# Two evictions per expert block: each half of layer 2 read out behind its own 24 matmuls

## Chip, cores and metric

The kernel runs on one core of one Trainium2 chip. The metric is device time in microseconds (us) of one execution; several executions are timed and their median counts. One further execution was recorded by the hardware profiler, and all rows below are of that one.

## What is computed

The input x is 8 batches of 2496 rows of 256 numbers. A two-dimensional Fourier transform is taken per batch and its real part kept, which gives 19968 rows (tokens). Each token goes to one of 8 experts, the one with the largest logit, and is written back at its own place:

```python
X = np.fft.fft(np.fft.fft(x, axis=1), axis=2).real
logits = X @ w_gate + modality_bias[modality_id]
e_idx = argmax(logits)                    # one expert per token
gate_w = softmax(logits)[e_idx]
out[mask] = gate_w[mask] * (relu(X[mask] @ w1[e]) @ w2[e])   # w1 256 x 1024, w2 1024 x 256
```

## The kernel before, in words

Two kinds of work share the engines. The **stream** makes the transform of one batch after the other (`fold`, `stage1`, `stage23`), computes the logits, gives each token a place in the list of its expert (`route`) and scatters the token rows to DRAM (`scatter`, line 726, an indirect DMA issued by GpSimd). The **expert blocks** (`block`, lines 1068 to 1153) take 256 rows (or, at the very end, 128 rows) of one expert from DRAM and run both layers on them. The first blocks run while the stream still makes later batches; later only blocks are left: first those of 256 rows, then those of 128.

A block of 256 rows does the following.

- **Loads**, issued by the sync engine: the expert's weights `w1` and `w2` (lines 1097, 1098, three slots each), the rows transposed as `xT` (line 1100, three buffers), and each row's place in the output and gate as `ig` (line 1103, four buffers).
- **Layer 1** (lines 1110 to 1127): four groups of 24 matmuls at 128 columns or, with 256 rows, of 12 matmuls at 256 columns; 48 matmuls in all. The three products of high and low fp16 parts are added up in a PSUM tile `psm` (three buffers). ScalarE writes the high part of the relu to `H` (line 1124), VectorE the low part (line 1125). `H` has two buffers.
- **Layer 2** (lines 1130 to 1140): for each half `tg` of 128 rows 24 matmuls at 256 columns into `po[:, tg, :]`. Both halves stand in one PSUM tile `pso` of 2 x 256 fp32 per partition, and the pool has one buffer for it (line 259).
- **Gates' product** `gs` (line 1144): one small VectorE instruction, held behind the block's own last relu instruction (`low`) by `issue_after`.
- **Eviction and scatter** (lines 1145 to 1152): for each half ScalarE reads `po[:, tg, :]`, multiplies by the gate and writes `ob` (four buffers), and GpSimd issues the indirect DMA that scatters `ob` to the output.

`block` is a generator. `blocks` and `spec_blocks` run the first part (loads, layer 1) of block b+1 ahead of the second part (layer 2, evictions) of block b, so the program's text has the order: layer 1 of b+1, layer 2 of b, layer 1 of b+2, layer 2 of b+1. `self.ob` is the last eviction issued in the text; the relu instructions of the next layer 1 in the text come behind it on ScalarE (lines 1122 to 1124).

The text's order is not the order on the engines. The kernel is built with

```python
    with tile.TileContext(nc, schedule_with_timeline_sim=True) as tc:
```

(line 1333): at build time a scheduler puts each engine's instructions in an order, by their place in the text and by estimated times at which their operands and buffers come free, and adds the semaphore waits that the accesses to each tile need. On the chip each engine then works through its fixed order. `issue_after` and `high_priority` are the kernel's means to bend that order.

Of the kernel before, what the change touches and what calls it, by code (L numbers as in the profile page):

```python
# [13 lines left out]
F32 = mybir.dt.float32  # L14
# [4 lines left out]
ALU = mybir.AluOpType  # L19
# [3 lines left out]
P = 128  # L23
B, N, D = 8, 2496, 256
TOK = B * N
E, F = 8, 1024
# [222 lines left out]
class Kernel:  # L249
# [818 lines left out]
    def block(self, S, ti, i, o=0, n=0, ex=None, slot=0, load=False):  # L1068

        keep = self.hold  # L1070
        self.hold = ()
        nc, t, p, tc = self.nc, self.t, self.mo, self.tc
        V = nc.vector
        NT = S // P
        ns = self.nslot
        sl = (self.off + i) % ns if ex is None else slot
        first = i < ns
        if ex is None:
            w = i % ns
            i = o + sum((n - j + ns - 1) // ns for j in range(w)) + i // ns  # L1080
        self.nblk += 1
        w1, w2 = self.w1[sl], self.w2[sl]
        kw = {}
        with ExitStack() as st:
            for x in keep + tuple(self.loads[-2:-1]):
                st.enter_context(tc.issue_after(x))
            ro = nc.sync.value_load(ti[0:1, 0, i:i + 1], min_val=0, max_val=DUMP)
            if ex is None:
                ee = nc.sync.value_load(ti[0:1, 1, i:i + 1], min_val=0, max_val=E - 1)
                if not first:  # L1090
                    kw = dict(cond=nc.sync.value_load(ti[0:1, 2, i:i + 1], min_val=0, max_val=1), cond_hint=False)
        if load:
            nc.sync.dma_start(w1, t["w16"][ex, :, 0:4 * F])
            nc.sync.dma_start(w2, t["w16"][ex, :, 4 * F:WROW])
        if ex is None:
            wsrc = t["w16"][ds(ee, 1)].rearrange("a p f -> (a p) f")
            nc.sync.dma_start(w1, wsrc[:, 0:4 * F], **kw)
            nc.sync.dma_start(w2, wsrc[:, 4 * F:WROW], **kw)
        xT = p.tile([P, 4, S], I16, name=f"xT{S}", tag="xT", bufs=3)
        r1 = nc.sync.dma_start_transpose(xT, t["xd"][ds(ro, S), 0:512])  # L1100
        xT = xT.bitcast(F16)
        ig = p.tile([P, NT, 2], F32, name=f"ig{S}", bufs=4)
        r2 = nc.sync.dma_start(ig.bitcast(I16), t["xd"][ds(ro, S), 512:516].rearrange("(t p) c -> p t c", p=P))
        self.loads.append(r2.ins)
        self.gather_dep(r1.ins)
        self.gather_dep(r2.ins)
        H = p.tile([P, 2, 8, S], F16, name=f"H{S}", tag="H", bufs=2)
        w1v = w1.rearrange("p (h k f) -> p h k f", h=2, k=2)
        NF = 512 // S
        for f0 in range(0, 8, NF):  # L1110
            ps = self.psm.tile([P, NF, S], F32, name="psm")
            for q in range(NF):
                ft = slice((f0 + q) * P, (f0 + q + 1) * P)
                k = 0
                for h, kt, xs in ((0, 0, 0), (0, 0, 2), (1, 0, 0), (0, 1, 1), (0, 1, 3), (1, 1, 1)):
                    with ExitStack() as st:
                        for x in keep:
                            st.enter_context(tc.issue_after(x))
                        l1 = nc.tensor.matmul(ps[:, q, :], w1v[:, h, kt, ft], xT[:, xs, :], start=k == 0, stop=k == 5).ins  # L1119
                    k += 1  # L1120
            with ExitStack() as st:
                if self.ob is not None:
                    st.enter_context(tc.issue_after(self.ob))
                nc.scalar.activation(H[:, 0, f0:f0 + NF, :], ps, AF.Relu)  # L1124
            self.mark = V.scalar_tensor_tensor(H[:, 1, f0:f0 + NF, :], ps, 0.0, H[:, 0, f0:f0 + NF, :], ALU.max, ALU.subtract).ins  # L1125
            if S == 256 and f0 % 4 == 0:
                self.tick(self.mark)
        self.l1, low = l1, self.mark
        yield
        w2v = w2[:, 0:4 * F].rearrange("p (h f d) -> p h f d", h=2, d=D)  # L1130
        po = self.pso.tile([P, NT, D], F32, name="pso")
        for tg in range(NT):
            k = 0
            for ft in range(8):
                for hh, wh in ((0, 0), (0, 1), (1, 0)):
                    with ExitStack() as st:
                        if S == P and k == 0:
                            st.enter_context(tc.issue_after(self.l1))
                        nc.tensor.matmul(po[:, tg, :], H[:, hh, ft, tg * P:(tg + 1) * P], w2v[:, wh, ft, :], start=k == 0, stop=k == 23)  # L1139
                    k += 1  # L1140
        gs = p.tile([P, NT], F32, name=f"gs{S}", bufs=3)
        with ExitStack() as st:
            st.enter_context(tc.issue_after(low))
            V.tensor_scalar(gs, ig[:, :, 1], w2[:, 4 * F:4 * F + 2].bitcast(F32), None, ALU.mult)
        for tg in range(NT):
            ob = p.tile([P, D], F32, name="ob", bufs=4)
            self.ob = nc.scalar.activation(ob, po[:, tg, :], AF.Identity, scale=gs[:, tg:tg + 1]).ins  # L1147
            ins = nc.gpsimd.indirect_dma_start(  # L1148
                out=t["out"], out_offset=bass.IndirectOffsetOnAxis(ap=ig.bitcast(I32)[:, tg, 0:1], axis=0),
                in_=ob, in_offset=None, bounds_check=TOK - 1, oob_is_err=False).ins  # L1150
            tc.declare_no_dep(ins, group="out_w", reason="rows are disjoint")
            tc.add_to_no_dep_group("out_w", ins)
        yield
# [189 lines left out]
```

## Time and profile before

| what | value |
|---|---|
| median of 3 timed runs | 1066.68 us (1066.59 to 1068.08) |
| profiled execution, its own time | 1056.95 us |
| its span, first to last instruction | 1055.2 us |
| TensorE matmul (PE) busy | 1009.6 us, 96% of the span |
| VectorE (DVE), ScalarE (ACT), GpSimd (POOL) busy | 532.3, 468.1, 363.2 us |
| layer 2's matmuls (L1139) | 3864, 452.2 us busy |
| layer 1's matmuls (L1119) | 4368, 457.7 us busy |
| evictions (L1147) | 161, 68.7 us busy |
| output scatters (L1148) | 161, 160.5 us busy on POOL |

How to read it: an engine is busy while an instruction of its own executes; PE, DVE, ACT and POOL work side by side, and SP issues most DMAs. Matmuls are pipelined: the start-to-start distance of two in a row is less than the duration given for one, so the time of a run of matmuls is read from the start of its first to the start of what follows. In a row of the timeline the bracket gives how long the engine stood idle before, and which instruction of which engine released it; a row without a bracket followed the one before it without a pause worth a mention. "x36" means 36 instructions in a row.

### The profile page before, as it was taken

The numbers are of one execution on the slowest core, as the hardware profiler recorded it, in microseconds if no ns is written. First come the engines' busy times: TensorE is split into PE (matmuls) and PEld (weight loads), VectorE is DVE, ScalarE is ACT, GpSimd is POOL, SyncE is SP. The second block draws the span as 40 slices with busy tenths as digits, with TensorE's granted clock in tenths as the row PEclk, the third lists the DMA queues.
The fourth block names the chain that finished last, engine by engine and source line by source line (L and its number), as shares of the span: only waits on it lengthen the run. The fifth ranks groups of instructions, "written<-read, shape, count | busy, mean of one in ns | idle before, by whom it ended". The sixth has DMA issues, their size and how long they took to land.

```text
span 1055.2 us, 25891 instructions
## 1 busy us (share of the span) xinstructions
PE 1009.6 (96%) x9910; PEld 906.9 (86%) x9910; DVE 532.3 (50%) x1567; ACT 468.1 (44%) x910; POOL 363.2 (34%) x353
## 2 busy tenths in 40 slices
PE   6979999999999998999999999999999999999996
PEld 6858778898899887988998898888888888898896
DVE  2848857577785576667654346522222222222221
ACT  4765566465555456436443334242323232332232
POOL 0066831227414444443333333444443121221111
PEclk9999999999999999999999999999999999999999
DMA  9836948458448949679764883789678887495972
GB/s 325 321 122 199 381 121 293 102 168 294 154 108 278 294 162 301 200 253 303 230 197 142 234 226 97 203 229 291 186 224 232 250 258 203 135 289 133 252 199 38
DMA packets 149724, 227.64 MB, mean 216 GB/s; under 512 B 116309, under 2 KB 117375, under 8 KB 132695
## 3 DMA queue, kind: packets, MB, share of 16 engines
q1 hardware_dynamic: 133031, 183.75, 60.2%
q0 software_dynamic: 16560, 42.15, 11.0%
q8 instruction: 80, 1.31, 0.5%
q14 instruction: 53, 0.43, 0.1%
HBM read 191.77 MB, written 62.48 MB: 241 GB/s over the span
## 4 chain that ended last, share of the span: by engine, by line
PE 74%; issue 11%; DMA 6%; POOL 3%; ACT 2%; DVE 2%; another core or an unknown queue 1%; SPq 0%; POOLq 0%; ACTq 0%
PE pso L1139 32%; PE psm L1119 32%; DMA XM<-x 3%; POOL out L1148 2%; DMA wa<-w 2%; PE psf L591 2%; PE psf L547 2%; PE psf L578 2%; PE psf L573 2%; PE psf L544 1%; PE psf L593 1%; DMA pack<-c_pack 1%; POOL xd L726 0%; DVE XM L405 0%
## 5 line engine op out<-in xcount | busy, mean ns | idle before, releaser
L1119 PE MATMUL psm<-xT,w 128*128 128x256 f16 (+1 forms) x4368 | 457.7, 261 | 8.0 <-DVE H L1125 2.8
L1139 PE MATMUL pso<-w,H 128*128 128x256 f16 x3864 | 452.2, 273 | 4.6 <-issue 2.4
L1119 PEld LDWEIGHTS <-w 128*128 128x128 f16 x4368 | 384.7, 98 | 50.0 <-issue 7.7
L1139 PEld LDWEIGHTS <-H 128*128 128x128 f16 x3864 | 375.0, 98 | 52.0 <-issue 9.2
L1125 DVE SCALAR_TENSOR_TENSOR H<-psm,H 128x512 f16<-128x512 f32 x322 | 219.3, 688 | 358.0 <-ACT H L1124 289.4
L1148 POOL DMA_INDIRECT out<-ob,ig x161 | 160.5, 997 | 499.2 <-ACT ob L1147 470.3
L1124 ACT ACTIVATE H<-psm 128x512 f16<-128x512 f32 x322 | 189.6, 597 | 256.0 <-PE psm L1119 186.5
L1147 ACT ACTIVATE ob<-pso,gs 128x256 f32<-128x256 f32 x161 | 68.7, 470 | 189.9 <-PE pso L1139 165.0
L726 POOL DMA_INDIRECT xd<-rp,dsti x88 | 101.6, 1155 | 114.6 <-DVE rm L233 49.8
L726 POOL DMA_INDIRECT xd<-rm,dsti x88 | 92.3, 1048 | 61.4 <-issue 20.8
L525 DVE SCALAR_TENSOR_TENSOR T<-psf,T 120x280 f16<-120x280 f32 (+2 forms) x95 | 43.4, 464 | 36.0 <-ACT T L524 35.2
L897 DVE SCALAR_TENSOR_TENSOR w<-wa,wsc,w 128x512 f16<-128x512 f32 (+1 forms) x52 | 42.5, 867 | 9.8 <-ACT w L890 9.6
L524 ACT ACTIVATE T<-psf 120x280 f16<-120x280 f32 (+2 forms) x95 | 38.7, 423 | 13.6 <-PE psm L1119 5.3
L578 PE MATMUL psf<-m2u,T 128*120 128x280 f32 x132 | 38.4, 414 | 2.3 <-ACT T L520 0.9
L547 PE MATMUL psf<-c,XM 128*128 128x132 f32 x240 | 31.9, 295 | 7.3 <-DMA c<-c_c 7.0
L591 PE MATMUL psf<-T,pack 120*128 120x145 f16 x330 | 34.5, 224 | 4.0 <-ACT T L524 1.6
L547 PEld LDWEIGHTS psf<-c,XM 128*128 128x128 f32 x240 | 30.7, 206 | 7.6 <-DMA XM<-x 7.0
L890 ACT ACTIVATE w<-wa,wsc 128x1024 f16<-128x1024 f32 (+1 forms) x24 | 33.4, 1426 | 2.2 <-DVE wsc L413 1.0
L525 DVE SCALAR_TENSOR_TENSOR rp<-psf,rp 128x256 f16<-128x256 f32 x55 | 22.9, 417 | 19.5 <-ACT rp L524 12.3
L573 PE MATMUL psf<-pack,T 128*120 128x144 f16 x330 | 31.9, 229 | 0.7 <-issue 0.7
L520 ACT COPY T<-psf 120x280 f32<-120x280 f32 (+2 forms) x57 | 22.7, 409 | 20.5 <-PE psf L578 9.3
L593 PE MATMUL psf<-T,pack 120*128 120x145 f32 (+1 forms) x132 | 24.1, 306 | 6.3 <-ACT T L520 3.7
(189 smaller groups left out, 611.3 us busy)
## 6 DMA issues: line engine op xcount, KB each, us to landing
w<-w SPq DMA_DIRECT2D x80, 1028.0 KB
w<-w SPq DMA_DIRECT2D x80, 1024.0 KB
XM<-x SPq DMA_DIRECT2D x14, 1280.0 KB
wa<-w SPq DMA_DIRECT2D x16, 1024.0 KB
out<-ob,ig POOLq DMA_INDIRECT x161
XM<-x SPq DMA_DIRECT2D x2, 768.0 KB
xT<-xd SPq DMA_TRANSPOSE x91
xd<-rp,dsti POOLq DMA_INDIRECT x88
```

Source lines behind the costliest of these rows:

```text
L525: self.mark = self.nc.vector.scalar_tensor_tensor(dst[:, 1], ps, scale, dst[:, 0], ALU.mult, ALU.subtract).ins
L547: self.staged = nc.tensor.matmul(o, src[:, k, i0 + i, :], self.c1[:, i1 + i, :], start=k == 0, stop=k == 1).ins
L573: nc.tensor.matmul(oh, T1[h][:, a, g, :], self.m2h[h][:, w], start=h + k == 0, stop=h * k == 2, skip_group_check=True)
L578: nc.tensor.matmul(ps[0:120, 0:280], T1[h][:, g, :], self.m2u[h], start=h == 0, stop=h == 1)
L591: nc.tensor.matmul(ps3[0:P, cols], self.e3h[:, a, j, :], T2[:, w, cols], start=k == 0, stop=k == 2)
L726: i = self.nc.gpsimd.indirect_dma_start(out=self.t["xd"], out_offset=bass.IndirectOffsetOnAxis(ap=at, axis=0), in_=row, in_offset=None, bo ...
L1119: l1 = nc.tensor.matmul(ps[:, q, :], w1v[:, h, kt, ft], xT[:, xs, :], start=k == 0, stop=k == 5).ins
L1124: nc.scalar.activation(H[:, 0, f0:f0 + NF, :], ps, AF.Relu)
L1125: self.mark = V.scalar_tensor_tensor(H[:, 1, f0:f0 + NF, :], ps, 0.0, H[:, 0, f0:f0 + NF, :], ALU.max, ALU.subtract).ins
L1139: nc.tensor.matmul(po[:, tg, :], H[:, hh, ft, tg * P:(tg + 1) * P], w2v[:, wh, ft, :], start=k == 0, stop=k == 23)
L1147: self.ob = nc.scalar.activation(ob, po[:, tg, :], AF.Identity, scale=gs[:, tg:tg + 1]).ins
L1148: ins = nc.gpsimd.indirect_dma_start(out=t["out"], out_offset=bass.IndirectOffsetOnAxis(ap=ig.bitcast(I32)[:, tg, 0:1], axis=0), in_=ob, i ...
```

## The change

The gates' product is written ahead of layer 2, and the second loop over the halves is gone: eviction and scatter of a half stand in the loop that makes it, behind its own 24 matmuls and ahead of those of the other half. No instruction is added or taken away. In a block of 128 rows there is one half only, and nothing but the place of the gates' product changes.

```diff
         w2v = w2[:, 0:4 * F].rearrange("p (h f d) -> p h f d", h=2, d=D)
         po = self.pso.tile([P, NT, D], F32, name="pso")
+        gs = p.tile([P, NT], F32, name=f"gs{S}", bufs=3)
+        with ExitStack() as st:
+            st.enter_context(tc.issue_after(low))
+            V.tensor_scalar(gs, ig[:, :, 1], w2[:, 4 * F:4 * F + 2].bitcast(F32), None, ALU.mult)
         for tg in range(NT):
             k = 0
             for ft in range(8):
...
                         nc.tensor.matmul(po[:, tg, :], H[:, hh, ft, tg * P:(tg + 1) * P], w2v[:, wh, ft, :], start=k == 0, stop=k == 23)
                     k += 1
-        gs = p.tile([P, NT], F32, name=f"gs{S}", bufs=3)
-        with ExitStack() as st:
-            st.enter_context(tc.issue_after(low))
-            V.tensor_scalar(gs, ig[:, :, 1], w2[:, 4 * F:4 * F + 2].bitcast(F32), None, ALU.mult)
-        for tg in range(NT):
             ob = p.tile([P, D], F32, name="ob", bufs=4)
             self.ob = nc.scalar.activation(ob, po[:, tg, :], AF.Identity, scale=gs[:, tg:tg + 1]).ins
             ins = nc.gpsimd.indirect_dma_start(
```

## Rows read from the trace of the kernel before

**Rows 1.** The page's busy time: engine, us, share of the span, instructions.

```profile
PE 1009.6 (96%) x9910; PEld 906.9 (86%) x9910; DVE 532.3 (50%) x1567; ACT 468.1 (44%) x910; POOL 363.2 (34%) x353
```

**Rows 2.** Stages: length, busy PE, PEld, DVE, ACT, POOL; granted clock; DMA share, GB/s.

```profile
100.00:600.00 500.00, 482.24 (x4689) 430.46 (x4689) 330.58 (x982) 262.21 (x515) 200.98 (x191) 0.99 0.72 224
...
700.00:900.00 200.00, 200.00 (x1835) 179.26 (x1833) 56.31 (x98) 62.30 (x116) 67.12 (x69) 1.00 0.82 234
```

**Rows 3.** Timeline, one block's cycle: start, length, engine, line, operation, tiles, count, idle before.

```profile
801.63 4.09 PE L1119 MATMUL psm<-xT,w 128*128 128x256 f16 x36
...
803.83 0.69 DVE L1125 SCALAR_TENSOR_TENSOR H<-psm,H 128x512 f16<-128x512 f32 x1 [2.99 <-ACT H L1124]
...
805.57 1.15 PE L1139 MATMUL pso<-w,H 128*128 128x256 f16 x9
...
806.55 1.47 PE L1119 MATMUL psm<-xT,w 128*128 128x256 f16 x12
...
807.86 4.42 PE L1139 MATMUL pso<-w,H 128*128 128x256 f16 x39
...
809.30 0.22 DVE L1144 TENSOR_SCALAR gs<-ig,w 128x2 f32<-128x2 f32 x1
...
812.12 4.09 PE L1119 MATMUL psm<-xT,w 128*128 128x256 f16 x36
...
812.37 0.84 ACT L1147 ACTIVATE ob<-pso,gs 128x256 f32<-128x256 f32 x2 [3.71 <-PE pso L1139]
...
813.12 0.97 POOL L1148 DMA_INDIRECT out<-ob,ig  x1 [8.23 <-ACT ob L1147]
```

**Rows 4.** Lines 1144 and 1147: forms of the gates' product; what ended ScalarE's idle time.

```profile
L1144 DVE TENSOR_SCALAR gs<-ig,w x91: 204/220/378, 107.5 to 1042.9; 128x2 f32<-128x2 f32 x70, 128x1 f32<-128x1 f32 x21
...
  PE pso L1139: 165.0, 66
```

**Rows 5.** Timeline, the last two blocks of 128 rows.

```profile
1041.49 2.78 PE L1139 MATMUL pso<-w,H 128*128 128x256 f16 x24
...
1044.31 0.47 ACT L1147 ACTIVATE ob<-pso,gs 128x256 f32<-128x256 f32 x1 [2.02 <-PE pso L1139]
1044.84 2.78 PE L1139 MATMUL pso<-w,H 128*128 128x256 f16 x24 [0.56 <-ACT ob L1147]
```

**Rows 6.** Timeline, first block: PE, then ACT; last a window's row, columns as rows 2.

```profile
114.46 0.38 PE L1139 MATMUL pso<-w,H 128*128 128x256 f16 x2
...
118.86 2.12 PE L1139 MATMUL pso<-w,H 128*128 128x256 f16 x14 [1.44 <-ACT ob L1147]
120.78 2.75 PE L1119 MATMUL psm<-xT,w 128*128 128x256 f16 x12
...
117.99 0.82 ACT L1147 ACTIVATE ob<-pso,gs 128x256 f32<-128x256 f32 x2
...
120.80:123.30 2.50, 2.50 (x13) 1.74 (x12) 2.50 (x10) 2.12 (x4) 1.92 (x2) 0.50 1.04 337
```

**Rows 7.** Timeline, three late evictions: layer 2's last matmuls, then their eviction.

```profile
351.44 4.42 PE L1139 MATMUL pso<-w,H 128*128 128x256 f16 x39
...
358.78 0.82 ACT L1147 ACTIVATE ob<-pso,gs 128x256 f32<-128x256 f32 x2
...
411.00 1.80 PE L1139 MATMUL pso<-w,H 128*128 128x256 f16 x15
...
415.46 0.82 ACT L1147 ACTIVATE ob<-pso,gs 128x256 f32<-128x256 f32 x2
...
652.99 1.91 PE L1139 MATMUL pso<-w,H 128*128 128x256 f16 x16
...
657.98 0.82 ACT L1147 ACTIVATE ob<-pso,gs 128x256 f32<-128x256 f32 x2
```

**Rows 8.** PE's waits over the whole span: us in total, times, longest.

```profile
PE psm L1119 <- DVE H L1125: 2.8, 2, 2.5
```

## The prediction

> **What bounds the kernel now.** I read the page first: TensorE is busy for 1009.6 us of the 1055.2 us span, twice as long as any other engine [rows 1]. A share over the whole span hides stages, so next come the windows. From 700 to 900 us, where only blocks of 256 rows run, PE is busy 200.00 us of 200 [rows 2]: nothing that shortens ScalarE's or GpSimd's work can be felt there. From 100 to 600 us, with the stream beside the blocks, PE stands idle for 500 - 482.24 = 17.8 us [rows 2]; that is all there is to gain, apart from the start and the end, which the change doesn't touch.
>
> The timeline of one cycle [rows 3] gives the order on PE: 36 matmuls of layer 1, 9 of layer 2, 12 of layer 1, 39 of layer 2, and again from 812.12, so 812.12 - 801.63 = 10.49 us for 96 matmuls, 0.109 us each, with no gap. Two things are to be seen in it. The first half's 24 matmuls are the 9 and 15 of the 39; they end at about 807.86 + 15 x 0.109 = 809.5. Yet ScalarE, idle for 3.71 us, starts the first eviction only at 812.37, behind the 48th matmul, and then does both in 0.84 us. So the program's guards treat `pso` as one thing: a reader waits for every matmul written ahead of it, whichever half it makes.
>
> **The change, part by part.** Reckoned on the profiled execution's own 1056.95 us; the median of the timed runs, 1066.68, lies 9.73 above it, and I add that difference at the end. About 0.2% (2.1 us) is what a measurement here can tell from no change.
>
> *Gates' product moved ahead of layer 2.* In the cycle it runs at 809.30 for 0.22 us, 3 us ahead of the eviction at 812.37, on a VectorE that is busy 56.31 us of 200 [rows 2, 3]. In both texts it waits for the block's own last relu, not for layer 2: 0. Its reader comes up to 2.8 us earlier, at 809.6, and 809.52 is still in time; without that cover at most its 0.22 us would add to each first eviction, less than what covers the boundary (below).
>
> *Scatter moved.* The first half's indirect DMA can leave GpSimd some 2.6 us earlier; GpSimd stood idle 8.23 us before it [rows 3], and no PE time hangs on it. The token scatters on the same queue may change places with it; each takes as long as before. 0. SyncE issues nothing new; the slots of `w2`, `ig` and `H` come free when the second half ends, later by whatever is put between the halves, some 1.3 us. What waits for them is for later blocks, with two to four buffers and a cycle of 10.49 us each: 0; without that cover the 1.3 us would show per block.
>
> *The eviction moved between the halves: a new wait.* By the same guard the second half's first matmul, now written behind the first half's eviction, must wait for it, since both are on `pso`. The product has 70 forms of two columns and 21 of one [rows 4], so there are 70 such boundaries. Its price stands at the kernel's end, where the last two blocks have nothing between them: 24 matmuls, eviction at 1044.31 for 0.47 us, the next 24 at 1044.84, PE idle 0.56 us [rows 5]. The 24 behind it take 2.78 us, as those before: this gap doesn't lower the clock. Queued behind the waiting matmul is all of PE's work, so an uncovered boundary costs 0.56 us: from 0 to 70 x 0.56 = 39 us.
>
> What covers it is layer 1 of block b+2: in the cycle it starts at 812.12 without a wait, so its rows and weights are there, and I take it that they are 2.6 us sooner too; `psm` has three buffers. That the build-time order pulls later work into a wait it foresees is in the cycle: the 9 matmuls of layer 2 ahead of layer 1's last 12 stand where it expected `psm` to be full. It overestimates such chains: VectorE had freed that buffer at 803.83 + 0.69 = 804.52, over 1 us before the 36 were through [rows 3]. A chain of one eviction should get 0.56 / 0.109 = 6 matmuls at least, and rather one group of 12 (1.31 us). I take **0 for the pure block stage**, being nearest to that row.
>
> In the mixed stage ScalarE isn't always free. Of 91 blocks 66 found it idle and waiting for PE [rows 4]; in the others it came from other work. The four latest first evictions, counted from layer 2's last matmul: 114.84 to 117.99 (3.15) [rows 6], 355.86 to 358.78 (2.92), 412.80 to 415.46 (2.66), 654.90 to 657.98 (3.08) [rows 7]. Before, 48 matmuls of layer 2 and then 36 of layer 1 (3.9 us) ran without that eviction; only in the first did PE wait for it, 1.44 us, and the 12 matmuls after that pause took 2.75 us, against 1.47 for 12 in the cycle [rows 3, 6]: the granted clock was 0.50 there, 1.2 instead of 2.4 GHz. With the change an eviction that late stands between the halves. Beyond a cover of 1.31 the four cost 1.84 + 1.61 + 1.35 + 1.77 = 6.6 us, and if each also drops the clock, 4 x (2.75 - 1.47) = 5.1 more: bounds 0 and 11.7. A gain is not excluded (below). I take half of 6.6, 3.3 us, as an estimate: ScalarE's order is written anew with this eviction in it, and part of the work that held it will come behind.
>
> Sum: 0 + 0 + 0 (block stage) + 3.3 = +3.3, 1060.25 us for a profiled run, **1070.0 us** on the median's scale.
>
> **A rule weighed.** The trace shows an eviction of one half waiting for the matmuls of the other [rows 3]. The Trainium skill, "PSUM — Partial Sum Buffer", section "PSUM bank collisions raise a hardware error", says that TensorE and ScalarE may not be on one bank of the same partitions at once, disjoint columns included, and advises to read another bank while matmuls run. The trace agrees, as far as the 2.87 us from 809.5 to 812.37 tell. By the rule alone each boundary stops PE, the second rival's 39 us; by the cycle's row it is filled, 0.
>
> **The rivals.** *All covered, nothing measurable*, 1066.7: the mixed stage's evictions find other filler too, the stream's matmuls. For it: 66 of 91 on time. Against: the four late ones.
>
> *The boundary is not filled*: PE stops 0.56 us 70 times, 1066.7 + 39 = 1106. It decides if the order puts no layer-1 matmul between the halves. For it: the guard [rows 3, 5]. Against: the 9 matmuls pulled forward.
>
> *Faster*: ScalarE no longer does 0.84 us of evictions in a row; behind the second half 0.47 is left, so relu and `psm` come 0.37 us sooner. If that, and a first eviction at 110 us rather than 118, removes the waits on `psm` (2.8 us) [rows 8] and on `pso` with its slow matmuls (1.44 + 1.28) [rows 6], 5.5 us go: 1061.2. It decides where ScalarE reaches the first eviction before its long operations. Against: it needs ScalarE exactly where it was late.
>
> *It doesn't do what it says*: with other work ahead in ScalarE's order the first eviction still comes behind the whole of layer 2. Then nothing moves; counted in the first rival.
>
> **How the numbers follow.** Small loss 0.33, all covered 0.32, not filled 0.10, faster 0.25. Slower by over 0.2% is 0.33 + 0.10 = 0.43, within 0.2% 0.32, faster 0.25. The forecast is the small loss, 1070.0. Its own upper bound is 1066.7 + 11.7 = 1078.4, and the lesser late ones that I didn't sum lie beyond it, so I end the range at 1080; downward it reaches to the faster case, 1061.5. Left out are the unfilled boundaries (0.10) and gains beyond 5 us (under 0.10).
>
> **What would show it.** In the timeline of 700 to 900 us: 24 matmuls of layer 2, about 12 of layer 1, 24 of layer 2, each eviction alone, 0.47 us behind its half, PE still 200.00 busy, the cycle still 10.49. In PE's waits: `pso` on ScalarE's `ob`, a handful of times between 100 and 660 us, a few us in total; many short ones of 0.56 mean the second rival. A lower PE idle from 100 to 600 than 17.8 means the faster one. I am wrong at the root if the second half starts while its neighbour is being read, or if the cycle changes.

## The result and the profile after

The changed kernel takes 1082.94 us (median of four runs, 1079.64 to 1084.78) against 1067.38 for the kernel before (four runs on the same chip, 1066.59 to 1069.95): the ratio is 1.0141, 95% interval 1.0098 to 1.0183. The change costs 15.6 us where 3.3 was forecast, and the time lies above the range's upper end of 1080. Measured twice more, on two chips, the loss was 0.9% and 1.0% (below). The sign was right, the size not.

The page's busy time of the changed kernel, the answer to [rows 1]:

```profile
span 1081.2 us, 25863 instructions
...
PE 1012.3 (94%) x9910; PEld 906.4 (84%) x9910; DVE 526.1 (49%) x1567; ACT 460.8 (43%) x910; POOL 357.3 (33%) x353
```

The same instructions, and PE busy for only 2.7 us more: the loss is for the most part not work but PE standing still. The stages, with the columns of [rows 2]:

```profile
100.00:600.00 500.00, 462.82 (x4494) 410.68 (x4493) 320.58 (x969) 250.56 (x498) 187.51 (x182) 0.98 0.69 212
...
700.00:900.00 200.00, 199.05 (x1820) 177.59 (x1818) 56.66 (x108) 60.57 (x118) 69.03 (x71) 1.00 0.82 239
```

From 700 to 900 us PE is busy nearly as before (199.05 against 200.00, and 15 matmuls fewer, about 1.6 us at 0.109 each). From 100 to 600 us it is idle for 500 - 462.82 = 37.2 us, where it was 17.8 [rows 2]. So the pure block stage all but carried the change, and the stage in which stream and blocks share the engines did not.

A cycle of the pure block stage, PE and then ScalarE, to hold against [rows 3]:

```profile
761.35 2.78 PE L1143 MATMUL pso<-w,H 128*128 128x256 f16 x24
763.97 1.36 PE L1119 MATMUL psm<-xT,w 128*128 128x256 f16 x11
765.17 2.78 PE L1143 MATMUL pso<-w,H 128*128 128x256 f16 x24
767.79 2.89 PE L1119 MATMUL psm<-xT,w 128*128 128x256 f16 x25
770.52 1.25 PE L1143 MATMUL pso<-w,H 128*128 128x256 f16 x10
...
764.22 0.47 ACT L1146 ACTIVATE ob<-pso,gs 128x256 f32<-128x256 f32 x1 [4.20 <-issue]
...
769.30 0.47 ACT L1146 ACTIVATE ob<-pso,gs 128x256 f32<-128x256 f32 x1 [3.15 <-PE psm L1119]
```

Counted through the trace, 24 by 24, the run at 761.35 is the second half of one block and that at 765.17 the first half of the next; the eleven of layer 1 stand between two blocks. Between the halves of a block stand 25: from 767.79 until the second half's first matmul at 770.52. The first half is through at 767.95 (765.17 + 2.78), its eviction begins at 769.30 and is over at 769.77, 0.75 us before the second half starts. That is the forecast's picture with twice its fill; behind the forecast's 12 matmuls, 1.31 us, PE would have waited for an eviction that comes so late. From the 48th block on 21 of 23 boundaries between halves have 25 matmuls in them, the other two 31.

PE's waits over the whole span, in us, times and longest, first those of before that stand beside [rows 8], then after:

```profile
PE psm L1119 <- DMA w<-w: 2.4, 2, 1.3
PE pso L1139 <- issue: 2.4, 5, 1.1
...
PE pso L1139 <- ACT ob L1147: 2.0, 2, 1.4
PE psm L1119 <- issue: 1.7, 3, 0.8
```

```profile
PE pso L1143 <- issue: 13.3, 9, 10.3
PE psm L1119 <- issue: 8.0, 12, 1.1
PE psm L1119 <- DVE H L1125: 6.9, 6, 1.7
...
PE pso L1143 <- ACT ob L1146: 4.8, 7, 1.1
PE psm L1119 <- DMA w<-w: 4.2, 3, 1.7
```

Three waits that the profile can name grew: `pso` on the eviction from 2.0 to 4.8, `psm` on VectorE's relu from 2.8 [rows 8] to 6.9, `psm` on weights from 2.4 to 4.2, together 8.7 us. "Issue", time for which the profile shows no releaser, grew from 11.1 to 27.0 over all lines. The largest piece of it is one stop, on PE, ScalarE and VectorE at once, in the timeline of 113 to 132 us (behind it a window's row, columns as [rows 2]):

```profile
130.42 0.97 POOL L726 DMA_INDIRECT xd<-rm,dsti  x1 [0.30 <-issue]
130.69 0.47 ACT L1146 ACTIVATE ob<-pso,gs 128x256 f32<-128x256 f32 x1 [15.05 <-remote]
...
131.22 1.65 PE L1143 MATMUL pso<-w,H 128*128 128x256 f16 x7 [10.28 <-issue]
...
131.69 0.69 DVE L1125 SCALAR_TENSOR_TENSOR H<-psm,H 128x512 f16<-128x512 f32 x1 [11.43 <-issue]
```

```profile
131.22:135.22 4.00, 4.00 (x21) 2.84 (x20) 1.38 (x5) 1.47 (x3) 2.12 (x3) 0.55 0.30 111
```

The 24 matmuls that this eviction reads were over by 116.9, and it comes 13.8 us later, while GpSimd goes on issuing token scatters. PE goes on just behind it, and its seven matmuls then take 1.65 us; seven take 0.92 in a row further below (at 479.88). The last row is the window of PE's first 4 us after the stop: the granted clock is 0.55, near the lower of its two levels (1.2 of 2.4 GHz), after 10 us in which PE stood still.

One caution on the scale. The profiled execution of before, 1056.95 us, lies 10.4 below its runs' median, that of after, 1082.95, on its own. Their difference of 26 us overstates the 15.6 of the medians, so a second pair of profiles is compared below. It is from two chips, on which the kernel before ran alike (medians 1044.16 and 1043.44).

### The profile page after: what moved, and what is told of

The parts are those of the page before. It is cut to its first block, busy times and chain, and to the rows that moved or that the text cites. A ratio compares the mean times of both kernels' runs of the same rounds, so it can differ in the third digit from the quotient of the medians.

```text
span 1081.2 us, 25863 instructions
## 1 busy us (share of the span) xinstructions
PE 1012.3 (94%) x9910; PEld 906.4 (84%) x9910; DVE 526.1 (49%) x1567; ACT 460.8 (43%) x910; POOL 357.3 (33%) x353
## 3 DMA queue, kind: packets, MB, share of 16 engines
q8 instruction: 80, 1.31, 0.5%
## 4 chain that ended last, share of the span: by engine, by line
issue 30%; PE 21%; POOL 10%; DMA 3%; DVE 1%; POOLq 1%; another core or an unknown queue 0%; ACT 0%; SPq 0%
PE psm L1119 9%; PE pso L1143 9%; POOL out L1147 7%; POOL xd L726 3%; DMA XM<-x 2%; PE psf L573 1%; PE psf L591 1%; DMA xT<-xd 1%; DMA xd<-rp,dsti 1%; PE psf L544 1%; POOLq L1147 0%; ACT H L1124 0%; DVE XM L405 0%; DVE H L1125 0%
## 5 line engine op out<-in xcount | busy, mean ns | idle before, releaser
L1119 PE MATMUL psm<-xT,w 128*128 128x256 f16 (+1 forms) x4368 | 463.4, 260 | 21.8 <-issue 8.0
L1143 PE MATMUL pso<-w,H 128*128 128x256 f16 x3864 | 462.6, 273 | 18.8 <-issue 13.3
L1125 DVE SCALAR_TENSOR_TENSOR H<-psm,H 128x512 f16<-128x512 f32 x322 | 215.1, 686 | 409.9 <-ACT H L1124 346.2
L1124 ACT ACTIVATE H<-psm 128x512 f16<-128x512 f32 x322 | 183.4, 596 | 173.9 <-PE psm L1119 111.4
L1146 ACT ACTIVATE ob<-pso,gs 128x256 f32<-128x256 f32 x161 | 76.0, 472 | 302.5 <-PE pso L1143 184.3
L726 POOL DMA_INDIRECT xd<-rm,dsti x88 | 88.2, 1002 | 49.3 <-issue 18.7
L573 PE MATMUL psf<-pack,T 128*120 128x144 f16 (+1 forms) x330 | 32.7, 229 | 1.9 <-DVE T L525 1.3
L524 ACT ACTIVATE rp<-psf 128x256 f16<-128x256 f32 x55 | 21.3, 387 | 20.7 <-remote 5.7
```

Of the source, the lines that this page charges most:

```text
L524: self.acted = self.nc.scalar.activation(dst[:, 0], ps, AF.Identity, scale=scale).ins
L573: nc.tensor.matmul(oh, T1[h][:, a, g, :], self.m2h[h][:, w], start=h + k == 0, stop=h * k == 2, skip_group_check=True)
L726: i = self.nc.gpsimd.indirect_dma_start(out=self.t["xd"], out_offset=bass.IndirectOffsetOnAxis(ap=at, axis=0), in_=row, in_offset=None, bo ...
```

## The experiments

**Where the loss is made.** The kernel before once more (no edit), as the base on the second chip:

> The kernel before, unchanged, to have a second profile of it: the first profiled execution took 1056.95 us, the timed ones 1066.6 to 1070.0. Theory A (the changed kernel loses by the first half's eviction coming late behind other ScalarE work in the mixed stage) says nothing on that gap. Theory B (most of the loss is one stop of ScalarE, VectorE and TensorE of 10 to 15 us near 116 us, which comes and goes between executions): the second profile of the kernel before lies near 1067 and shows a stop of about 10 us near 116 us that the first one lacks. If it lies near 1057 again without such a stop, the timed executions differ from the profiled ones for a reason outside the trace.

1044.08 us, ratio 0.9994 (0.9969 to 1.0019). Its profile is compared below with that of the change on a third chip. The gates' product alone moved, the two evictions left where they were:

```
+        gate()
         for tg in range(NT):
             ...
-        gs = p.tile(...); V.tensor_scalar(gs, ...)
```

> Only the gates' product is moved ahead of layer 2, both evictions stay behind all 48 matmuls. Theories A and B: within 2 us of before, since its reader and the wait on pso are as before. Rival C (the moved product takes VectorE's time from the relu of the next block): 3 us or more slower.

1.0013 (0.9987 to 1.0040): it costs nothing that can be measured. Next the whole change in a part of the blocks, with the old order in the others:

```
+SPLIT = lambda n: n > 47        # the other run: n <= 47
...
+            if SPLIT(me):
+                evict(tg)
+        if not SPLIT(me):
+            for tg in range(NT):
+                evict(tg)
```

> The change only in blocks from the 48th on, where the stream is over (from about 660 us). Theories A and B: the boundary is filled with layer 1's matmuls, so within 2 us of before (the changed kernel has 1 us more idle PE from 700 to 900 us). Rival D (each boundary stops PE for 0.56 us): 22 blocks, 12 us slower.

> The change only in the first 47 blocks, those beside the stream. Theories A and B: as slow as the whole change, 13 to 16 us slower than before. By A the loss is spread: 9 us more idle PE from 200 to 700 us in single waits of 0.3 to 2 us on pso and psm; by B 10 us or more of it stand in one stop near 116 us.

In the blocks from the 48th on 1.0002 (0.9977 to 1.0026), in the first 47 alone 1.0063 (1.0044 to 1.0083): 7 us, half of the 13 to 16 expected. The loss is made in the mixed stage. Compared one by one, operation and tile, PE's first 6310 of 9910 matmuls stand in the first run in the order of the kernel before and in the second in that of the whole change, so the parting of the blocks didn't bring a third order into that stage.

**The change again.** No edit, on the third chip and later on a fourth:

> The changed kernel, unchanged, beside runs of the kernel before on the same chip. The part for the first 47 blocks alone cost 0.63% and the part behind them nothing. Theory A (ScalarE late for the first half's eviction in the mixed stage, and nothing else): 0.4 to 0.9% slower here. Theory B (a stop of 10 us near 116 us belongs to the changed order): 1.2 to 1.6% slower, with that stop in the profile.

> The changed kernel once more, beside the three above on the same chip. If the time of the change depends on the chip only by the stop of 10 us and more at 116 us that its first profile showed: 0.9% slower than before (0.6 to 1.2) where the profile has no such stop, about 1.4% where it has.

On the third chip 1052.07 against 1043.44 us: 1.0088 (1.0063 to 1.0113). On the fourth 1079.01 against 1066.69: 1.0103 (1.0068 to 1.0138). The intervals overlap with that of the first measurement. The three profiles of the change have one and the same order of operations and tiles on every engine, and so have the two of the kernel before: what differs from chip to chip isn't the order. Neither new profile has one stop at 116 us, but on the fourth chip PE stands idle under "issue" in twelve pieces between 110 and 137 us, 10.0 us in all. PE's waits, the kernel before on the second chip and then the change on the third:

```profile
PE psm L1119 <- DMA xT<-xd: 5.8, 1, 5.8
PE psm L1119 <- DVE H L1125: 5.7, 3, 4.9
PE pso L1139 <- ACT ob L1147: 2.0, 2, 1.4
PE psm L1119 <- DMA w<-w: 1.9, 2, 1.2
```

```profile
PE psm L1119 <- DVE H L1125: 8.5, 7, 1.9
PE psm L1119 <- DMA xT<-xd: 6.7, 2, 6.1
PE pso L1143 <- ACT ob L1146: 4.9, 7, 1.2
PE psm L1119 <- DMA w<-w: 4.2, 3, 2.6
```

No "issue" here in either. The four differences are 2.8 + 0.9 + 2.9 + 2.3 = 8.9 us, and the spans differ by 1051.9 - 1043.6 = 8.3. So on these chips the loss is these four waits. What stands in front of two of them is plain in the timeline. For `pso`, PE and ScalarE of the change:

```profile
471.56 2.78 PE L1143 MATMUL pso<-w,H 128*128 128x256 f16 x24 [1.25 <-ACT ob L1146]
...
479.88 0.92 PE L1143 MATMUL pso<-w,H 128*128 128x256 f16 x7 [1.06 <-ACT ob L1146]
...
476.81 0.89 ACT L229 COPY rm<-rp 128x774 f16<-128x774 f16 x1
...
478.80 0.67 ACT L230 ACTIVATE rm<-rp 128x508 f16<-128x508 f16 x1
479.32 0.51 ACT L1146 ACTIVATE ob<-pso,gs 128x256 f32<-128x256 f32 x1
```

The first half is through at 474.34 (471.56 + 2.78); its eviction stands behind a row of the stream's copies on ScalarE until 479.32, and PE stands behind the eviction. That is the forecast's mechanism. But not all of these waits are of that kind. The seven are, besides these two and 0.56 at the kernel's end, which the kernel before has too:

```profile
175.64 2.78 PE L1143 MATMUL pso<-w,H 128*128 128x256 f16 x24 [0.53 <-ACT ob L1146]
...
334.98 1.25 PE L1143 MATMUL pso<-w,H 128*128 128x256 f16 x10 [0.76 <-ACT ob L1146]
...
402.37 2.78 PE L1143 MATMUL pso<-w,H 128*128 128x256 f16 x24 [0.30 <-ACT ob L1146]
...
651.89 2.34 PE L1143 MATMUL pso<-w,H 128*128 128x256 f16 x20 [0.40 <-ACT ob L1146]
```

Counted through the trace, those at 175.64, 334.98 and 479.88 stand between the halves of a block, 2.35 us together. Those at 402.37, 471.56 and 651.89 stand in front of a block's first half, which waits for the block before's second eviction, 1.95 us together. And the kernel before's wait of 1.44 us in the first blocks [rows 6] is gone. For `psm`, PE and VectorE of the change:

```profile
236.87 1.36 PE L1119 MATMUL psm<-xT,w 128*128 128x256 f16 x11 [0.86 <-DVE H L1125]
...
233.99 1.56 DVE L405 TENSOR_TENSOR XM<-XM 128x768 f32<-128x768 f32 x2 [2.62 <-DMA XM<-x]
235.47 0.42 DVE L232 COPY rm<-rp 128x774 f16<-128x774 f16 x1
235.81 0.41 DVE L233 TENSOR_SCALAR rm<-rp 128x762 f16<-128x762 f16 x1
236.14 0.68 DVE L1125 SCALAR_TENSOR_TENSOR H<-psm,H 128x512 f16<-128x512 f32 x1
```

Here the relu that would free a `psm` buffer stands on VectorE behind three pieces of the stream's work, the first of which waited 2.62 us for its own load. The prediction has no term for this.

**Two guesses at what makes it.** First, that the wait on `pso` comes from the two halves lying in one bank. A bank of its own for each half needs a bank from the stream (`psf`), so the kernel before with three `psf` buffers is its control:

```
-        self.psf = pool("psf", 4, space=PSUM)
+        self.psf = pool("psf", 3, space=PSUM)
...
-        self.pso = pool("pso", 1, space=PSUM)
+        self.pso = pool("pso", 2, space=PSUM)
...
-        po = self.pso.tile([P, NT, D], F32, name="pso")
+        po = [self.pso.tile([P, D], F32, name="pso") for _ in range(NT)]
```

> The changed kernel with a pso tile of its own, in a bank of its own, for each half (two buffers in the pool); the bank comes from psf, which has three buffers in place of four. So the second half's matmuls need not wait for the first half's eviction. Theory A: the waits of PE on pso's eviction in the mixed stage go (5.1 us in the run with the early blocks alone) and it is no slower than the kernel before with three psf buffers, within 0.3%. Rival E (the loss comes from layer 1 pulled in between the halves, which fills psm early, or from ScalarE's order): it stays 0.5% or more slower than that control.

> Control for the two banks: the kernel before with three psf buffers in place of four. The stream's stages have one bank less: 0 to 1.5% slower than before by either theory; it is what the two-bank kernel is to be compared with.

1.0271 (1.0229 to 1.0313) with two banks and 1.0233 (1.0183 to 1.0282) for the control, 0.4% apart with some 0.7% of uncertainty. In the profiles the waits of `pso` on `ob` go from 5.6 us in the control to 1.0, so they do hang on the shared bank, but those of `psf` grow and the bank itself costs over 2%. What the shared bank's wait is worth in time stays undecided: the nearer control, the changed kernel with three `psf` buffers, ran on another chip only (below).

Second, that the relu of the fill is held by the second half's eviction, behind which the program ties it. Tied behind the first half's instead:

```
-            self.ob = nc.scalar.activation(...).ins
+            e = nc.scalar.activation(...).ins
+            if tg == 0:
+                self.ob = e
```

> The changed kernel, with the relu of the next layer 1 held behind the first half's eviction in place of the second's on ScalarE, so that layer 1 pulled in between the halves can be evicted at once. Rival E (psm filled early and not emptied is what costs: waits of PE on psm of 1.7 us each): 2 us or more faster than the changed kernel. Theory A: within 2 us of the changed kernel, since the late first evictions stay late.

1.0085 (1.0054 to 1.0116), as the change without it. But the two traces have the same order of operations and tiles on every engine, one by one: the tie doesn't shape the order, and this run is the change once more. Whether the relu would gain by another place wasn't tested.

**Late blocks, or the order?** In the profile of the change on the third chip ten blocks had a first eviction that came 1.4 to 5.1 us behind its matmuls. The change in all blocks but these, and in these alone:

```
+SPLIT = lambda n: n not in (1, 3, 5, 6, 8, 9, 10, 18, 19, 29)   # and: n in (...)
```

> The change in all blocks but ten (numbers 1, 3, 5, 6, 8, 9, 10, 18, 19 and 29): those whose first half's eviction came 1.4 to 5.1 us behind its 24 matmuls in the profile of the changed kernel, while the others' came at once. Theory A (the loss is made where ScalarE is late for the first half): most of the loss goes, no more than 0.4% slower than before, and waits of pso on ob under 2 us in all. Rival (the loss comes from the new order and from buffers that come free later, in whichever block): 0.7 to 1.0% slower, as the whole change.

> The mirror of the run before: the change in those ten blocks alone. Theory A: 0.5% or more slower than before, waits of pso on ob 3 us or more. Rival: 10 of 91 blocks should give about a tenth of the loss, 0.1%, no difference that can be measured.

Without the ten the loss stays, 1.0083 (1.0066 to 1.0099); the ten alone cost 1.0008 (0.9974 to 1.0043). My theory A fell in this form. The profiles tell why: without the ten PE still waits for `ob` for 5.6 us, seven times, the longest, 2.6 us, at 268 us, where the whole change on this chip has no such wait; and with the ten alone it waits 0.6. Which block's eviction is late isn't a property of the block. The order is the same each time one text is built, but it is written anew for each text, and the stream's work falls before other evictions. Without the ten the wait for relu is only 1.5 us and the loss is there all the same.

The run with the ten alone, 0.1% off the kernel before, also gives a pair of profiles from one chip, the fourth. From it to the whole change the waits for `ob` go from 0.6 to 4.8 us, for relu from 1.1 to 7.2, for weights from 1.9 to 2.7, for `xT` from 2.3 to 2.7: 11.5 us of the spans' 1079.0 - 1066.2 = 12.8. "Issue" goes from 20.6 to 23.0, and between 110 and 140 us both have some 10 us of it, so that idle time comes without the loss too.

**The boundary left bare.** In the changed kernel, layer 1 of the 256-row blocks from the 49th on is held behind the last layer-2 matmul written ahead of it. That puts PE's order in those cycles back to 36, 9, 12, 39, with the eviction inside the 39:

```
+        wall = self.l2 if S == 256 and self.nblk > 48 else None
...
+                        if wall is not None:
+                            st.enter_context(tc.issue_after(wall))
                         l1 = nc.tensor.matmul(...)
...
+                        self.l2 = nc.tensor.matmul(po[:, tg, :], ...).ins
```

> The changed kernel with layer 1 of each 256-row block from the 49th on held behind the last layer-2 matmul that is written ahead of it, so that PE's order there is again that of before (36, 9, 12, 39) and nothing of layer 1 stands between the halves. If the cover at the boundary is what makes the pure block stage free: each of some 22 boundaries shows PE waiting for ob for about 0.56 us, the cycle of two halves grows from 10.49 to about 11.05 us, PE's busy share in 700 to 900 us falls to about 95%, and the kernel is 12 us (1.1%) slower than the changed one. Rival (the boundary costs nothing even bare, since the second half may start while the first is read): no idle time there, cycle 10.49, time as the changed kernel.

1.0278 (1.0219 to 1.0336), 1098.64 us: 19.6 above the change on the same chip. The timeline of a cycle, PE and ScalarE, and then PE's waits between 690 and 930 us:

```profile
761.29 1.80 PE L1147 MATMUL pso<-w,H 128*128 128x256 f16 x15
763.70 2.78 PE L1147 MATMUL pso<-w,H 128*128 128x256 f16 x24 [0.61 <-ACT ob L1150]
766.32 4.09 PE L1123 MATMUL psm<-xT,w 128*128 128x256 f16 x36
...
763.17 0.47 ACT L1150 ACTIVATE ob<-pso,gs 128x256 f32<-128x256 f32 x1
```

```profile
PE pso L1147 <- ACT ob L1150: 12.3, 20, 1.0
```

Seventeen of these twenty waits are 0.61 us each, one at every boundary of a held block, and three more like them lie behind 930 us: 20 x 0.61 = 12.2 us, where the forecast's price was 0.56 each [rows 5]; PE's busy time in 700 to 900 us falls from 198.94 to 188.94. That is the second rival's mechanism, and what keeps it away is the fill. The other 7 us aren't explained by this edit; the profile has a stop of 12.0 us before 131 us, as the first profile of the change has.

**More buffers for `psm`?** If `psm` runs out because relu is late, a fourth buffer should end it. The bank comes from `psf` again, so both kernels are run with three `psf` buffers, once with three and once with four of `psm`:

```
-        self.psf = pool("psf", 4, space=PSUM)
-        self.psm = pool("psm", 3, space=PSUM)
+        self.psf = pool("psf", 3, space=PSUM)
+        self.psm = pool("psm", 4, space=PSUM)
```

> Control: the kernel before with three buffers of psf in place of four, so that a PSUM bank is free. About 2.3% slower than before, as measured earlier. The pair of this and the next gives the change's price at three psm and three psf buffers; both theories expect 0.6 to 1.2% between them.

> The changed kernel with three buffers of psf. Both theories: 0.6 to 1.2% above the kernel before with three psf buffers (3.0 to 3.5% above before), with waits of psm on H of 6 us or more and of pso on ob of 4 to 6 us.

> The kernel before with the free bank given to psm: four psm buffers, three of psf. Waits of psm on H 1 us or less; as the before with three psf buffers or a little faster, by no more than 0.3%, since psm on H cost it only some 3 us.

> The changed kernel with four psm buffers and three of psf. Theory B (psm's buffers run out because relu comes late): waits of psm on H fall from 7 to 2 us or less and the price of the change, against the kernel before with the same buffers, falls to 0.5% or less. Rival (order, pso and the rest): the price stays at 0.7 to 1.2%, whatever psm has.

Against the same runs of before: 1.0197 (1.0143 to 1.0251) and 1.0126 (1.0073 to 1.0178) with three, 1.0188 (1.0132 to 1.0243) and 1.0147 (1.0099 to 1.0194) with four. All four ran on a fifth chip. So with three `psf` buffers the change costs -0.7%, with four of `psm` -0.4%, each uncertain by some 0.7%. Both theories had expected a loss in the first pair, and there is none. The runs on this chip scatter by 1%, too much to say that the change helps there; the profiled ones too, the changed kernel with three at 1083.58 against its median of 1075.12, with four at 1068.02 against 1076.96. The wait on relu did go with the fourth buffer, to 0.2 us in the changed kernel, but it was only 1.3 with three.

**Stirring the order.** One VectorE operation of two columns per block in the first 47 blocks, of no use, makes the order come out anew:

```
+            if self.nblk < 48:
+                V.tensor_scalar(p.tile([P, 2], F32, name="gz", bufs=2)[:, 0:NT], ig[:, :, 1], 1.0, None, ALU.mult)
```

> The kernel before with one more VectorE operation of two columns, of no use, ahead of the gates' product in the first 47 blocks: about 0.24 us each on an engine that has room, so 0 by its own weight. If the order alone moves the time (theory C): 0.2% or more off before, to either side. If not: within 0.2%.

> The changed kernel with the same operation. If the loss is the split's own (theory D): 0.7 to 1.4% slower than the run before this one. If it belongs to one order (theory C): anything from 0.5% faster to 1.5% slower than it, and not the 0.9% again save by chance.

On the third chip the kernel before stays where it was, 1.0000 (0.9983 to 1.0017); the changed one comes to 1.0047 (1.0027 to 1.0066). The same change costs about half of what it cost on that text, less than the 0.7% that a loss of the split's own was expected to keep. PE's waits in the two, before and change:

```profile
PE psm L1119 <- DVE H L1125: 5.8, 4, 4.6
PE psm L1119 <- DMA xT<-xd: 5.6, 1, 5.6
PE psm L1119 <- DMA w<-w: 2.2, 3, 1.3
...
PE pso L1139 <- ACT ob L1149: 0.6, 1, 0.6
```

```profile
PE psm L1119 <- DMA xT<-xd: 7.3, 3, 6.6
...
PE pso L1145 <- ACT ob L1148: 5.0, 7, 1.2
PE psm L1119 <- DVE H L1125: 5.0, 2, 4.8
PE psm L1119 <- DMA w<-w: 4.3, 3, 3.1
```

The wait for `ob` is up by 4.4 us, that for weights by 2.1, that for `xT` by 1.7, and that for relu is down by 0.8. Set side by side, the rise of each wait from the kernel before to the changed one (us in the profiles; the price is the ratio of the timed runs):

| pair | `ob` | weights | relu | price |
|---|---|---|---|---|
| first chip | 2.0 to 4.8 | 2.4 to 4.2 | 2.8 to 6.9 | +1.4% |
| second and third chip | 2.0 to 4.9 | 1.9 to 4.2 | 5.7 to 8.5 | +0.9% |
| fourth chip, from ten blocks to all | 0.6 to 4.8 | 1.9 to 2.7 | 1.1 to 7.2 | +0.9%, +-0.5 |
| stirred order | 0.6 to 5.0 | 2.2 to 4.3 | 5.8 to 5.0 | +0.5% |
| three `psf` | 3.6 to 6.5 | 1.6 to 3.3 | 4.2 to 1.3 | -0.7%, +-0.7 |
| three `psf`, four `psm` | 2.7 to 6.1 | 1.7 to 4.3 | none to 0.2 | -0.4%, +-0.7 |

Two columns rise in every pair: the wait for the eviction by 2.8 to 4.4 us, that for weights by 0.8 to 2.6. Together that is about 5 us, 0.5%: what I take for the change's own price, and the stirred pair's 0.5% fits it. It is read from single profiles, and those of one text differ: the kernel before with three `psf` buffers waited 5.6 and 3.6 us for `ob` and 2.8 and 1.6 for weights on two chips. So the rise for weights isn't clear of the scatter; the gates' product alone had 2.7 there. The relu column goes either way with the order. In the last two pairs the timed runs show no loss although both columns rise; whether the order there gives it back elsewhere or the scatter of that chip hides it stays open, and so does how much of any one price is order. In no pair is the change clearly faster.

## Why the prediction was wrong in its size

**Pure block stage, 0: right.** The fill is there (25 matmuls between the halves where about 12 were forecast), the eviction of 0.47 us lies beside it, and PE was busy for 200.00 of 200 us on the third chip. The bare boundary's price holds, 0.61 against 0.56, and so does the reading of the guard: the second half does wait for its neighbour's reader. The runs price the program's guard: where nothing fills the boundary it stops PE, and here it is filled. The rule of the Trainium skill, "PSUM — Partial Sum Buffer", section "PSUM bank collisions raise a hardware error", that TensorE and ScalarE may not be on one bank at once, wasn't put to the test, since the guard keeps them apart in every run.

**Gates' product, 0: right**, 1.0013 with an interval around 1. **The doesn't-do-what-it-says rival** is out: each half's eviction does come behind its own 24.

**Mixed stage, late first evictions, +3.3: right in place, and in size by luck.** PE's waits for `ob` rose by 2.8 and 2.9 us in the two pairs. But the forecast counted how late an eviction is from layer 2's last matmul, and in the changed order PE needs it from the end of the first half, 24 matmuls or 2.6 us sooner: counted so, the latest came 5.1 us late on the third chip, not 3.15. Its cover was mis-sized the other way: at the wait of 479.88 PE had run for 4.5 of the 5.5 us since the first half's end, on layer 1 and the stream, not for 1.31. The two nearly cancel, and no wait between two halves of a block passed 1.06 us there. Of the rise of 2.9 us, 2.35 is the forecast's wait, 1.95 the next block's first half behind a late second eviction, which the forecast didn't have, less the 1.44 that its *faster* rival expected to go. Halving 6.6 was a guess, and the blocks named from [rows 6, 7] weren't to be relied on.

**What failed is the sum, which had only that term.** "SyncE issues nothing new; the slots ... come free later ...: 0" was short by some 2 us: the wait for weights rose by 1.8 and 2.3 us. All of it lies behind 930 us, in the stage of 128-row blocks. That it is the slots' 1.3 us handed on isn't shown: with the change in the late blocks alone it was 2.9 us, with the gates' product alone 2.7. And `psm` was given no price at all ("`psm` has three buffers"), save as a gain in the *faster* rival, which had relu come 0.37 us sooner. Instead relu's wait rose by 4.1 and 2.8 us. This step, the wait of layer 1 for VectorE put at nothing, is the largest that failed. The prediction noted that 36 matmuls of layer 1 had stood behind a late eviction without harm, and 39 of layer 2 in a row; it didn't ask what that long row of layer 2 was good for. Once its `H` is written it needs nothing more of VectorE, so VectorE may be 4.4 us late behind it; behind a half of 24 only 2.78. That this shorter reserve is why relu breaks through in three of the pairs is my reading of the timeline and isn't shown; the stirred pair, the run without the ten blocks and those with three `psf` buffers, where it doesn't, speak for an order that happens to be good or bad.

**On the first chip** a stop of 10.3 us came on top, in PE's "issue". Its cause stays open. Profiles of changed texts have it in one piece (10.3 us, 12.0 in the held one, 5.6 without the ten blocks) or in many (10.0 us in pieces of at most 1.8 when the change was measured again), and the profile names no releaser. The run with the ten blocks alone has 10.8 us of it between 110 and 140 us at a price of 0.1%, so it need not belong to the change; the first profile of before, which lay 10.4 us below its runs, has 2.5 there. What makes the first measurement's excess over the 0.9 to 1.0% of the others can't be told from profiles of single executions, and their intervals overlap.

**The range** ended at 1080 since it took only the late evictions' bound, 11.7. With the measured rises for relu and weights on top, 4.1 + 1.8, it would have ended at 1084.3 and held 1083.

## What to carry to other kernels

When a change splits a long run of PE work that depends on no other engine, price not only the new wait at the cut but what that run was covering: each engine's lateness, each buffer and each load that came due behind it. In a stage whose order is written by a program, don't take a single late block for the cause; take the waits by kind, before and after, and stir the order with an idle operation to see which kinds belong to the change. An experiment that needs a buffer from another pool is worth nothing without the kernel before run with the same buffers.

## What was not expected of the hardware

The same kernel before ran at 1043 to 1044 us on two chips and at 1062 to 1067 on others, and the slower chips' profiles have PE's idle time under "issue", with no releaser (11 us in the first profile of before, added over its lines), where those from the faster chips list none. And in the pure block stage, with one and the same order, the first halves' evictions came 0.04 to 0.09 us behind their matmuls on the third chip, but 0.7 to 2.1 us behind on the first (blocks 49 to 56); ahead of the one at 769.30 ScalarE stood idle for 3.15 us. One fewer of the stream's four PSUM buffers costs 2.0 to 2.3%, more than the change. And in the stop at 116 to 131 us ScalarE, VectorE and PE resume within a microsecond of each other, at the last of eleven `rm` scatters that GpSimd issues in a row, though the trace shows none of them waiting for GpSimd; for ScalarE it says "remote", which no view resolves.
